# Loading batch 0's keys and queries in halves, and cutting the channel mix by free token tiles, in a fused attention and channel-mix kernel

## The chip, the core and the metric

The kernel runs on one NeuronCore of one Trainium2 chip. The core has a matrix engine (TensorE, PE in the profile; PEld is its weight load), a vector engine (VectorE, DVE), a scalar engine (ScalarE, ACT), a general engine (GpSimd, POOL) and a sync engine (SyncE, SP). Each works through its own queue of instructions in order, and they wait for each other through semaphores. In this kernel POOL's queue issues nearly all loads from memory, and SP's queue issues nearly all stores. The metric is device time in microseconds (us) of one execution, as the median of the runs shown.

## The reference

The inputs are q, k and v of shape 8 batches x 8 heads x 576 tokens x 64, phi of shape 8 x 8 x 576 x 32, and the weights of a channel mix. First comes an attention over 32 memory slots, then the channel mix over the 512 joined columns of each token:

```python
a = exp(phi - max(phi)); a = a / sum(a)                # over axis 2, the 576 tokens
k_m = einsum('bhsm,bhsd->bhmd', a, k)                  # 32 x 64 for each head
v_m = einsum('bhsm,bhsd->bhmd', a, v)
attn = softmax(q @ k_m.T / sqrt(64))                   # 576 x 32 for each head
x = join_heads(attn @ v_m)                             # batch, 576, 512
x_prev = x shifted by one token (zeros first)
xk = mu_k * x + (1 - mu_k) * x_prev                    # xr the same, with mu_r
key = relu(xk @ w_k) ** 2                              # 512 -> 1024
out = sigmoid(xr @ w_r) * (key @ w_v)                  # 1024 -> 512
```

## The kernel before

**The order of the work is written out by hand.** `PLAN` is a list of words, and the kernel emits its steps in just that order. Each engine therefore meets its instructions in the order of the words. A word such as `0:s1` is step `s1` of batch 0, `c0:3` is step 3 of the channel mix of chunk 0, and `p:wk:0-4` puts a load on POOL's queue.

**Attention of a batch.** `exp` turns phi into weights (ACT, L220). `k`, `v` or `kv` sum keys and values under them (72 matmuls with 64 or 128 columns, L232). `z` sums the weights (9 matmuls, L241). `nk` and `nv` divide by that sum (DVE). `tk` transposes the summed keys and `q0`, `q1` the queries, on PE, and DVE or ACT copies each result out of PSUM. `s0` and `s1` are the scores of two groups of four heads, with an exponential on ACT (L322, L326). `l0` to `l3` sum the exponentials and take the logarithm. `h0z` to `h3z` (or `r0z`, `r1z`) take the exponential of its negative, and `y0` to `y3` (or `w0`, `w1`) multiply (DVE, L353). Batches 0 and 1 then use `nk0`, `nk1`, `nr0`, `nr1`: the summed values times `mu` and `1 - mu` (DVE, L396). `mk0`, `mk1`, `mr0`, `mr1` build the mixed rows xk and xr for tokens 0 to 319 (half 0) or 320 to 575 (half 1) by matmuls alone (L266), and ACT and DVE share the copies into `xkT` and `xrT` (L413). Later batches compute x (`x0`, `x1`), a difference (`dd`) and the mix (`k0d`, `k2d`, `r0d`, `r2d`) on ACT and DVE. `mub` spreads `mu` over the partitions with one fp32 matmul (L195). `busy7` is seven matmuls of zeros.

**Channel mix.** The 4608 tokens are cut into nine chunks of 512. Steps 0 to 7 of a chunk are keys: four matmuls of 512 columns (L484), a relu on ACT (L488) and a square on DVE into the chunk's own `sq` tile (two buffers). Steps 8 to 11 are gates, one for each 128 tokens: four matmuls (L498), an exponential, and after every second gate a logarithm and an exponential of both (L503, L505, L506). Steps from 12 on are values: eight matmuls against `wv` (L519), a product with the gate on DVE (L521) and the stores on SP (L465). Chunk 0's values are cut into column halves, because `wv` arrives in two column halves.

**Loads.** Before the plan starts, k of batch 0 is put on POOL's queue as two halves of 64 partitions (`load_parity`, L110), then the identity matrix is made on POOL. The plan's first `p:` words add q and v of batch 0 (also two halves each), then the first half of `wk`, phi of batch 1, `wr`, k of batch 1, the second half of `wk`, q and v of batch 1, and the two halves of `wv`. Each `load` step adds a batch two ahead. From batch 6 on the queries are transposed by DMA from SP's queue (`qx`).

Of the kernel before, what the change touches and what calls it, by code (L numbers as in the profile page):

```python
# [10 lines left out]
F32 = mybir.dt.float32  # L11
BF16 = mybir.dt.bfloat16
# [6 lines left out]
    "0:exp0 0:exp1 0:k 0:z 0:mub 0:nk p:q:0 0:q0 0:q1 0:tk 0:s0 0:s1 p:v:0 p:wk:0-4 0:v 0:nk1 0:nk0 0:mu 0:nr0",  # L19
    "p:phi:1 0:l2 p:wr:0-4 0:l1 p:k:1 0:h1z 0:y1 0:l3 0:h2z 0:y2 0:l0 0:nr1 0:h3z 0:busy7 0:h0z p:wk:4-8 0:y0 0:y3",  # L20
    "0:mk1 0:mk0 0:mr0 c0:1 1:exp 0:mr1 c0:2 p:q:1 p:v:1 c0:8 c0:10 c0:11 1:k 1:z 1:nk c0:4 1:tk p:wv:0-2 c0:7 c0:5",
    "1:q0 1:q1 c0:0 c0:3 1:s0 1:v 1:s1 c0:6 1:nr0 1:l2 p:wv:2-4 1:l3 1:nk0 1:l1 0:load 1:h1z 1:l0 1:nk1 1:h3z 1:h2z",
    "1:h0z 1:y1 c0:18 c0:9 1:nr1 c0:16 1:y2 1:y0 1:y3 c0:19 c0:17 1:mk0 1:mk1 c0:15 1:load 2:exp c1:4 c1:0 1:mr0 c1:1",
    "c1:5 2:z c1:2 c1:6 2:q1 c1:8 2:q0 c0:13 2:kv 2:nk 1:mr1 2:tk 3:exp c1:3 2:s1 2:s0 c1:7 2:nv c0:14 2:load 2:l0",
    "2:l3 2:l1 c0:12 2:r0z c2:8 2:w0 2:l2 2:r1z 2:w1 3:z c1:9 3:q1 3:q0 c1:12 2:x0 c1:13 2:x1 3:kv 4:exp 3:load 3:nk",
    "3:nv c1:10 3:tk 2:dd c1:11 2:k0d 2:k2d c1:14 3:s0 3:s1 c1:15 6:load 3:l0 c2:6 3:l1 3:l3 2:r0d 3:l2 c2:0 3:r0z",
    "3:w0 3:r1z 3:w1 c2:3 c2:5 c2:1 c2:2 4:z 3:x1 2:r2d c2:4 4:kv 4:nv 4:nk 3:x0 3:dd c2:7 3:k2d c2:10 5:exp c2:9",
    "4:tk 4:q1 4:q0 3:k0d 4:load c2:12 c2:11 c2:13 c2:15 5:z 4:s1 5:kv 5:nv 4:s0 5:q0 3:r0d 5:nk 6:exp 5:q1 c3:5 4:l2",
    "c3:8 c3:6 c3:3 4:l1 5:tk 4:l0 3:r2d c3:4 4:r0z 4:l3 c3:2 c3:0 c3:1 6:z 4:r1z 6:kv 6:nv 5:s0 4:w1 5:s1 c3:7 c3:9",
    "4:w0 c2:14 6:nk 5:load 4:x1 c3:12 7:load 4:x0 6:qx c3:10 5:l3 7:exp 6:tk 4:dd 5:l1 c3:11 5:l0 5:l2 4:k2d 5:r1z",  # L30
    "4:k0d 5:r0z c3:14 c3:15 c3:13 5:w0 5:w1 c4:8 c4:1 c4:5 7:z 4:r2d 5:x0 c4:7 7:kv 6:s1 7:nk 7:nv 6:s0 c4:4 c4:0",
    "6:l2 4:r0d c4:6 5:x1 6:l0 7:tk c4:2 c4:3 6:l3 6:l1 c4:10 c4:11 7:qx 5:dd 6:r1z 5:k0d 5:k2d 6:r0z 6:w1 6:w0 c4:14",
    "c4:9 c4:15 c4:12 5:r0d 6:x0 c4:13 6:x1 6:dd c5:2 6:k0d c5:8 6:k2d c5:3 c5:1 c5:4 c5:7 c5:5 c5:6 c5:0 7:s0 7:s1",
    "c6:3 c6:6 c5:9 7:l0 7:l1 5:r2d 6:r0d c6:4 7:l2 7:r0z c6:5 7:l3 c5:13 c5:12 c6:0 7:w0 7:r1z 7:w1 c5:10 c6:8 c6:2",
    "c6:1 6:r2d c6:7 7:x0 c5:11 c5:14 7:x1 c6:9 7:dd 7:k0d 7:k2d c6:13 c6:12 c5:15 c6:10 c6:11 c8:4 c6:15 c7:8 c7:9",
    "c8:1 c8:7 c6:14 7:r2d c7:3 c8:0 7:r0d c7:5 c7:6 c7:4 c7:0 c7:1 c7:2 c7:7 c7:10 c8:3 c8:5 c8:6 c7:13 c7:11 c7:12",
    "c8:2 c7:15 c8:8 c7:14 c8:9 c8:10 c8:11 c8:12 c8:13 c8:14 c8:15",
# [3 lines left out]
PRE = "k:0 id:"  # L41
# [7 lines left out]
def kernel(  # L49
# [26 lines left out]
    NCH = NTOK // CT  # L76
# [15 lines left out]
    zeros = const.tile([128, CT], BF16, name="zeros")  # L92
# [15 lines left out]
    def load_parity(dst, src):  # L108
        for r in ROWS:
            nc.gpsimd.dma_start(out=dst[r].rearrange("p h j d -> p h (j d)"), in_=rows(src)[r])  # L110
# [33 lines left out]
    def preload(word):  # L144

        what, _, part = word.partition(":")
        if what in weights:
            dst, src = weights[what]
            f0, f1 = (int(x) * 128 for x in part.split("-"))
            nc.gpsimd.dma_start(out=dst[:, :, f0:f1], in_=src[:, :, f0:f1])  # L150
        elif what == "id":
            make_identity(nc, identity)
        else:
            n = int(part)
            if what == "phi":
                load_phi(n, nc.gpsimd)
            else:
                dst = qs[n].rearrange("p (h j) d -> p h j d", j=NJ) if what == "q" else kvs[n][:, "kv".index(what)]
                (load_rows if n else load_parity)(dst, {"q": q, "k": k, "v": v}[what][n])
# [24 lines left out]
    xr_T = big.tile([128, ND, RING], BF16, name="xrT")  # L184

    def keep_busy(n):

        ps = psum.tile([128, CT], F32, name="idle", tag="ps", bufs=8)
        for _ in range(n):
            nc.tensor.matmul(ps, lhsT=zeros[:, 0:128], rhs=zeros, start=True, stop=True,  # L190
                             skip_group_check=True)
# [14 lines left out]
    def attention(b):  # L206
# [31 lines left out]
        def esum():  # L238
            st["zps"] = ps_tile([128, 2], F32, "zps")
            for j in range(NJ):  # L240
                nc.tensor.matmul(st["zps"], lhsT=em[:, j].rearrange("p h m -> p (h m)"), rhs=ones,  # L241
                                 start=j == 0, stop=j == NJ - 1, skip_group_check=True)
            st["rz"] = work.tile([128, 2], F32, name="rz", tag="rz", bufs=3)
            nc.vector.reciprocal(st["rz"], st["zps"])

# [45 lines left out]
        def cross_q():  # L291
            for hg in range(2):
                nc.sync.dma_start_transpose(out=q_tile()[:, hg],
                                            in_=qs[b % 2][ROWS[hg]].rearrange("p n d -> p (n d)"))

# [105 lines left out]
        def mixed(w, hf):  # L401

            def go():
# [7 lines left out]
                for i in range(ND):  # L411
# [6 lines left out]
                 "z": esum, "nk": norm_k(), "nv": norm_v, "tk": tr_k(), "load": reload, "mu": load_mu, "mub": load_mu_b, "qx": cross_q}  # L418
        for i in range(2):
            steps[f"q{i}"] = tr_q(i)  # L420
            steps[f"exp{i}"] = lambda i=i: exp_phi(slice(2 * i, 2 * i + 2))
# [48 lines left out]
    def channel_mix(c):  # L470
        t0 = c * CT
        wrap = RING - t0 % RING
        pieces = [(0, CT)] if wrap >= CT else [(0, wrap), (wrap, CT)]
        st = {}

        def key(fi):
            def go():
                if "sq" not in st:
                    st["sq"] = work.tile([128, NF, CT], BF16, name="sq", tag="sq", bufs=2)
                pk = psum.tile([128, CT], F32, name="pk", tag="ps", bufs=8)  # L480
                for lo, hi in pieces:
                    c0 = (t0 + lo) % RING
                    for di in range(ND):
                        nc.tensor.matmul(pk[:, lo:hi], lhsT=wk_sb[:, di, fi * 128:(fi + 1) * 128],  # L484
                                         rhs=xk_T[:, di, c0:c0 + hi - lo],
                                         start=(di == 0), stop=(di == ND - 1))
                rl = work.tile([128, CT], BF16, name="rl", tag="rl", bufs=3)
                nc.scalar.activation(rl, pk, AF.Relu)  # L488
                nc.vector.tensor_mul(st["sq"][:, fi, :], rl, rl)  # L489
            return go  # L490

        def gate(ts):

            def go():
                pr = psum.tile([128, Dm], F32, name="pr", tag="ps", bufs=8)
                c0 = (t0 + ts * 128) % RING
                for di in range(ND):
                    nc.tensor.matmul(pr, lhsT=xr_T[:, di, c0:c0 + 128],  # L498
                                     rhs=wr_sb[:, di, :], start=(di == 0), stop=(di == ND - 1))
                if ts % 2 == 0:  # L500
                    st[ts // 2] = work.tile([128, 2, Dm], F32, name="sg", tag="sg", bufs=2)
                sg = st[ts // 2]
                nc.scalar.activation(sg[:, ts % 2], pr, AF.Exp, scale=-1.0)  # L503
                if ts % 2 == 1:
                    nc.scalar.activation(sg, sg, AF.Ln, bias=1.0)  # L505
                    nc.scalar.activation(sg, sg, AF.Exp, scale=-1.0)  # L506
            return go

        def value(ts, hs=(0,), n=1):

            def go():
                if ("o", ts) not in st:
                    st["o", ts] = work.tile([128, Dm], F32, name="o", tag="o", bufs=4)
                o = st["o", ts]
                for h in hs:
                    cols = slice(h * Dm // n, (h + 1) * Dm // n)
                    pv = psum.tile([128, Dm], F32, name="pv", tag="ps", bufs=8)
                    for fi in range(NF):
                        nc.tensor.matmul(pv[:, cols], lhsT=st["sq"][:, fi, ts * 128:(ts + 1) * 128],  # L519
                                         rhs=wv_sb[:, fi, cols], start=(fi == 0), stop=(fi == NF - 1))  # L520
                    nc.vector.tensor_mul(o[:, cols], st[ts // 2][:, ts % 2, cols], pv[:, cols])  # L521
                    store(o, t0 // 128 + ts, cols)
            return go

        if c == 0:
            values = [value(ts, (h,), 2) for ts in range(4) for h in range(2)]
        elif c == NCH - 1:
            values = [value(ts) for ts in range(3)] + [value(3, (0, 1), 2)]
        else:
            values = [value(ts) for ts in range(4)]  # L530
        return [key(fi) for fi in range(NF)] + [gate(ts) for ts in range(4)] + values


    attend = [attention(b) for b in range(B)]
    mixes = [channel_mix(c) for c in range(NCH)]
    todo = []
    for n, word in enumerate(" ".join(PLAN).split()):
# [3 lines left out]
        elif who[0] == "c":  # L541
            todo.append((n, -1, word, mixes[int(who[1:])][int(name)]))
# [34 lines left out]
```

## Time and profile before

| what | value |
|---|---|
| median of three runs | 210.34 us (209.8 to 210.54) |
| the profiled execution's own time | 210.08 us |
| span of that execution, first to last instruction | 208.3 us |
| granted TensorE clock, mean | 0.996 |
| PE busy | 193.5 us, 93% of the span |
| ACT busy | 159.7 us, 77% |
| DVE busy | 132.8 us, 64% |
| first matmul of the mixed rows of batch 0 | 19.31 us |
| first matmul of the first value | 35.95 us |
| last matmul group ends, by the chain | 204.33 us |

Times inside the execution are counted from the span's start. Busy time is the union of an engine's instructions. The profiled execution is 1.8 us longer than its span (210.08 against 208.3), and this part lies before the first and after the last instruction. The chain that ended last is followed back from the last instruction to whatever released each step. A timeline row gives a start, the time covered, the engine, the line, the operation with its tiles, the shape and a count, and in brackets the idle time ahead of it with the instruction that ended it.

### The profile page before, as it was taken

Reading aid. Unit: us, or ns where it says so; the run is one execution under the profiler, and the core shown is the slowest. Engines: PE = TensorE matmul, PEld = TensorE weight load, DVE = VectorE, ACT = ScalarE, POOL = GpSimd, SP = SyncE. Lnnn points to the kernel's source line nnn. Section 1 sums busy time; section 2 is a strip of 40 time slices with the busy share of each in tenths; the row PEclk is TensorE's granted clock in tenths of the full one; section 3 lists DMA queues with packets and bytes.
Section 4 is the critical chain, followed back from the end, with each engine's and each line's share of the span. In section 5 each row is a group of like instructions: output and inputs, shape, how many; then the busy total and the mean of one; then the engine's idle time right before and its main releaser. Section 6 shows DMA issues by size and latency. Waiting matters only on the chain.

```text
span 208.3 us, 5501 instructions
## 1 busy us (share of the span) xinstructions
PE 193.5 (93%) x2242; PEld 99.6 (48%) x2242; DVE 132.8 (64%) x331; ACT 159.7 (77%) x306; POOL 29.4 (14%) x45
## 2 busy tenths in 40 slices
PE   0379999999999999999999999999999999999992
PEld 0344454755545445465445864444444444444451
DVE  2046634866567899897769789896664925743132
ACT  3146988983998899888998999869789498656570
POOL 7653222210504004140000000000000000000000
PEclk9999999999999999999999999999999999999998
DMA  6999999999999999999997840530040262104434
GB/s 161 166 207 261 207 208 203 259 236 279 212 274 227 275 269 223 250 250 286 209 193 140 175 43 0 129 77 0 0 107 0 50 151 63 41 0 98 101 69 134
DMA packets 29273, 32.47 MB, mean 156 GB/s; under 512 B 6704, under 2 KB 24384, under 8 KB 29248
## 3 DMA queue, kind: packets, MB, share of 16 engines
q0 software_dynamic: 17392, 20.91, 53.4%
q1 hardware_dynamic: 11088, 10.37, 22.1%
q10 hardware_dynamic: 768, 0.85, 1.3%
q8 instruction: 17, 0.28, 0.5%
q14 instruction: 8, 0.07, 0.1%
HBM read 38.28 MB, written 9.44 MB: 229 GB/s over the span
## 4 chain that ended last, share of the span: by engine, by line
PE 80%; DMA 15%; POOL 2%; DVE 1%; issue 1%; POOLq 0%
PE pv L519 30%; PE pk L484 27%; PE pr L498 14%; DMA wv<-in_moe_w_v_dram 10%; DMA kv<-in_v_dram 5%; PE kvps L232 2%; PE nops L266 1%; PE zps L336 1%; PE qtps L303 1%; PE scps L322 1%; POOL kv L110 1%; DVE o L521 1%; PE mxps L266 1%; PE zps L241 1%; POOL q L110 1%
## 5 line engine op out<-in xcount | busy, mean ns | idle before, releaser
L484 PE MATMUL pk<-xkT,wk 128*128 128x512 bf16 (+1 forms) x320 | 68.3, 358 | 0.2 <-DMA wk<-in_moe_w_k_dram 0.2
L519 PE MATMUL pv<-wv,sq 128*128 128x512 bf16 (+1 forms) x328 | 66.9, 353 | 0.4 <-DMA wv<-in_moe_w_v_dram 0.4
L488 ACT ACTIVATE rl<-pk 128x512 bf16<-128x512 f32 x72 | 42.6, 606 | 11.8 <-PE pk L484 9.7
L489 DVE TENSOR_TENSOR sq<-rl 128x512 bf16<-128x512 bf16 x72 | 29.8, 423 | 31.6 <-ACT rl L488 31.1
L519 PEld LDWEIGHTS <-sq 128*128 128x128 bf16 x328 | 31.3, 98 | 30.9 <-issue 1.2
L484 PEld LDWEIGHTS <-wk 128*128 128x128 bf16 x320 | 29.9, 98 | 28.7 <-issue 1.1
L521 DVE TENSOR_TENSOR o<-sg,pv 128x512 f32<-128x512 f32 (+1 forms) x41 | 24.6, 619 | 19.7 <-PE pv L519 12.9
L498 PE MATMUL pr<-wr,xrT 128*128 128x512 bf16 x144 | 35.5, 380 | 0.0
L503 ACT ACTIVATE sg<-pr 128x512 f32<-128x512 f32 x36 | 21.2, 602 | 11.8 <-PE pr L498 8.4
L498 PEld LDWEIGHTS <-xrT 128*128 128x128 bf16 x144 | 13.5, 98 | 15.0 <-ACT xrT L413 0.3
L505 ACT ACTIVATE sg<-sg 128x1024 f32<-128x1024 f32 x18 | 19.0, 1057 | 0.6
L506 ACT ACTIVATE sg<-sg 128x1024 f32<-128x1024 f32 x18 | 19.0, 1057 | 0.6
L232 PE MATMUL kvps<-kv,em 64*32 64x128 bf16 (+1 forms) x720 | 8.7, 218 | 8.7 <-DMA kv<-in_k_dram 8.5
L365 ACT CAST x<-nops 128x320 bf16<-128x320 f32 (+1 forms) x48 | 15.6, 412 | 1.4 <-PE nops L266 1.4
L387 DVE TENSOR_SCALAR mu_d<-diff,mu 128x576 bf16<-128x576 bf16 x48 | 15.7, 369 | 0.1
L353 DVE TENSOR_TENSOR atn<-e,lz 128x576 bf16<-128x576 bf16 (+2 forms) x20 | 12.1, 633 | 2.6 <-ACT lz L346 2.4
L341 ACT ACTIVATE lz<-zps 128x320 f32<-128x320 f32 (+1 forms) x32 | 12.1, 419 | 0.7 <-PE zps L336 0.6
L232 PEld LDWEIGHTS <-em 64*32 64x32 bf16 x720 | 7.3, 92 | 10.9 <-ACT em L220 5.6
L326 ACT ACTIVATE e<-scps 128x320 bf16<-128x320 f32 (+1 forms) x32 | 10.7, 417 | 1.9 <-PE scps L322 1.9
L220 ACT ACTIVATE em<-ph 128x1152 bf16<-128x1152 f32 (+1 forms) x9 | 9.5, 1067 | 2.3 <-DMA ph<-in_phi_dram 2.3
L346 ACT ACTIVATE lz<-lz 128x576 f32<-128x576 f32 (+2 forms) x20 | 11.1, 585 | 0.2
L106 POOL DMA_DIRECT2D kv<-in_k_dram x7 | 5.2, 741 | 39.0 <-PE kvps L232 17.9
(61 smaller groups left out, 145.9 us busy)
## 6 DMA issues: line engine op xcount, KB each, us to landing
out_dram<-o SPq DMA_DIRECT2D x61, 128.0 KB, 2.4
ph<-in_phi_dram POOLq DMA_DIRECT2D x7, 576.0 KB, 20.0
kv<-in_k_dram POOLq DMA_DIRECT2D x7, 576.0 KB, 14.6
q<-in_q_dram POOLq DMA_DIRECT2D x7, 576.0 KB, 18.3
kv<-in_v_dram POOLq DMA_DIRECT2D x7, 576.0 KB, 19.7
out_dram<-o SPq DMA_DIRECT2D x18, 64.0 KB, 5.2
wk<-in_moe_w_k_dram POOLq DMA_DIRECT2D x2, 512.0 KB, 14.6
wv<-in_moe_w_v_dram POOLq DMA_DIRECT2D x2, 512.0 KB, 20.6
```

The costliest lines, as they stand in the source:

```text
L232: nc.tensor.matmul(kvps[c][g * M:(g + 1) * M], lhsT=em[ROWS[c], j, g, :], rhs=kv5[ROWS[c], parts, g, j, :], start=j == 0, stop=j == NJ - 1 ...
L365: nc.scalar.copy(st["x"][:, i, sl], pss[i])
L387: nc.vector.tensor_scalar_mul(t[:, i], st["d"][:, pr + i, :], mu1[:, o:o + 1])
L484: nc.tensor.matmul(pk[:, lo:hi], lhsT=wk_sb[:, di, fi * 128:(fi + 1) * 128], rhs=xk_T[:, di, c0:c0 + hi - lo], start=(di == 0), stop=(di = ...
L488: nc.scalar.activation(rl, pk, AF.Relu)
L489: nc.vector.tensor_mul(st["sq"][:, fi, :], rl, rl)
L498: nc.tensor.matmul(pr, lhsT=xr_T[:, di, c0:c0 + 128], rhs=wr_sb[:, di, :], start=(di == 0), stop=(di == ND - 1))
L503: nc.scalar.activation(sg[:, ts % 2], pr, AF.Exp, scale=-1.0)
L505: nc.scalar.activation(sg, sg, AF.Ln, bias=1.0)
L506: nc.scalar.activation(sg, sg, AF.Exp, scale=-1.0)
L519: nc.tensor.matmul(pv[:, cols], lhsT=st["sq"][:, fi, ts * 128:(ts + 1) * 128], rhs=wv_sb[:, fi, cols], start=(fi == 0), stop=(fi == NF - 1))
L521: nc.vector.tensor_mul(o[:, cols], st[ts // 2][:, ts % 2, cols], pv[:, cols])
```

## The change

Five things change together.

1. **k and q of batch 0 are used half by half.** The load order on POOL becomes k first half, identity, q first half, k second half, q second half, v second half, v first half, phi of batch 1, `wk` first half, `wr`, `wk` second half, k, q and v of batch 1, `wv`. The summed keys are made for one half of the partitions at a time (`k0c`, `k1c`; `v0c`, `v1c` for the values), normalised and transposed for that half (`hn0`, `ht0`, `hn1`, `ht1`), and the queries of one half are transposed by themselves (`qh0`, `qh1`, new function `tr_q_rows`), so that `s0` needs only the first halves.
2. **Chunk 0 has 576 tokens**, and its keys are cut at token 320 (`c0:3a` is tokens 0 to 319, `c0:3b` tokens 320 to 575). The other chunks are seven of 512 and a last one of 448.
3. **Gates and values are numbered by token tile** (`g:0` to `g:35`, `o:0` to `o:35`) and stand anywhere in the plan. Tiles 0 to 3 keep their column halves (`o:3a`, `o:3b`).
4. **The squared keys live in one ring** of 1152 tokens (`sq`) in place of two chunk buffers. A chunk that crosses the ring's end squares in two pieces.
5. **The plan is new from the first word to the last**, with `busy4` for `busy7`. `zeros` shrinks to 128 columns, read four times over. The options `zr` and `hold` are defined and unused.

```diff
-    "0:exp0 0:exp1 0:k 0:z 0:mub 0:nk p:q:0 0:q0 0:q1 0:tk 0:s0 0:s1 p:v:0 p:wk:0-4 0:v 0:nk1 0:nk0 0:mu 0:nr0",
-    "p:phi:1 0:l2 p:wr:0-4 0:l1 p:k:1 0:h1z 0:y1 0:l3 0:h2z 0:y2 0:l0 0:nr1 0:h3z 0:busy7 0:h0z p:wk:4-8 0:y0 0:y3",
-    "0:mk1 0:mk0 0:mr0 c0:1 1:exp 0:mr1 c0:2 p:q:1 p:v:1 c0:8 c0:10 c0:11 1:k 1:z 1:nk c0:4 1:tk p:wv:0-2 c0:7 c0:5",
-    "1:q0 1:q1 c0:0 c0:3 1:s0 1:v 1:s1 c0:6 1:nr0 1:l2 p:wv:2-4 1:l3 1:nk0 1:l1 0:load 1:h1z 1:l0 1:nk1 1:h3z 1:h2z",
...
+    "0:exp0 0:exp1 0:z p:q:0a 0:k0c 0:qh0 0:hn0 p:k:0b p:q:0b 0:ht0 0:k1c 0:hn1 p:v:0b 0:s0 0:qh1 p:v:0a 0:ht1 0:l0",
+    "0:h0z 0:s1 0:mub p:phi:1 0:l1 0:y0 0:l3 p:wk:0-4 0:h3z 0:v1c 0:h1z 0:nk1 0:v0c 0:l2 0:y3 0:nr1 0:y1 0:nr0 0:nk0",
+    "0:busy4 0:h2z p:wr:0-4 0:y2 p:wk:4-8 0:mk1 0:mr1 c0:3b 0:mr0 1:exp 0:mk0 g:2 p:k:1 c0:0b g:3 c0:2a c0:7a g:0",
+    "c0:4b 1:z c0:3a 1:k 1:nk c0:2b 7:load c0:0a c0:1a c0:4a c0:6b p:q:1 p:v:1 1:tk 1:q1 1:q0 p:wv:0-2 c0:7b c0:5a",
+    "1:s1 c0:6a 1:v 1:s0 c0:5b c0:1b 1:l0 1:l1 1:nk0 1:l3 1:h3z 1:nk1 1:l2 1:h1z 1:h2z 1:nr1 1:h0z g:1 1:y3 0:mu o:3a",
+    "1:nr0 o:2a 1:y2 1:y1 p:wv:2-4 1:y0 o:2b o:3b 1:mk1 0:load o:1b 1:mk0 6:load 1:mr0 c1:7 c1:4 2:exp c1:6 c1:5 g:4",
...
+    "5:z 3:k2d 6:qx o:10 5:kv 4:s0 4:s1 5:nk o:9 5:nv 3:r0d c3:6 4:l1 4:l2 c3:4 c3:1 3:r2d 4:l0 c3:0 6:exp 5:q0 5:q1",
+    "g:12 5:tk 4:l3 c3:5 c3:3 4:r0z c3:7 6:z 6:kv 4:r1z 5:s1 4:w0 5:s0 4:w1 c3:2 g:13 6:nk 6:nv o:11 6:tk 4:x0 o:12",
+    "4:x1 g:14 5:l0 4:dd 5:load 5:l1 g:15 5:r0z 7:exp 5:l2 4:k2d 4:k0d 5:l3 5:r1z o:13 5:w0 o:15 o:14 c4:7 c4:0 7:z",
...
-PRE = "k:0 id:"
+PRE = "k:0a id:"
...
+    STARTS = (0,) + tuple(range(S, NTOK, CT))
...
+    sq = big.tile([128, NF, 2 * S], BF16, name="sq")
...
+        def tr_q_rows(hg):
+            def go():
+                r = ROWS[hg]
+                for i in range(2):
+                    ps = ps_tile([128, NJ, QR], BF16, "qtps")
+                    for n in range(NJ):
+                        n0 = 2 * (NJ * i + n)
+                        nc.tensor.matmul(ps[:, n], rhs=identity[r, r], is_transpose=True,
+                                         lhsT=qs[b % 2][r, n0:n0 + 2, :].rearrange("p n d -> p (n d)"),
+                                         start=True, stop=True, skip_group_check=True)
+                    (nc.scalar.copy if i else nc.vector.tensor_copy)(q_tile()[:, hg, NJ * i:NJ * (i + 1)], ps)
+            return go
...
+        def key(fi, lo, hi):
+            def go():
+                pk = psum.tile([128, CT], F32, name="pk", tag="ps", bufs=8)[:, :hi - lo]
+                cut = min(hi, -(lo + 1) // RING * -RING)
+                for p0, p1 in ((lo, cut), (cut, hi)) if cut < hi else ((lo, hi),):
...
                 nc.scalar.activation(rl, pk, AF.Relu)
-                nc.vector.tensor_mul(st["sq"][:, fi, :], rl, rl)
+                cut = min(hi, -(lo + 1) // (2 * S) * (-2 * S))
+                for p0, p1 in ((lo, cut), (cut, hi)) if cut < hi else ((lo, hi),):
+                    p = p0 % (2 * S)
+                    nc.vector.tensor_mul(sq[:, fi, p:p + p1 - p0], rl[:, p0 - lo:p1 - lo], rl[:, p0 - lo:p1 - lo])
...
+        if c == 0:
+            return {f"{fi}{'ab'[hf]}": key(fi, sl.start, sl.stop) for fi in range(NF) for hf, sl in enumerate(HALVES)}
...
+    def gate(t):
...
+            if t % 2 == 0:
+                gated[t // 2] = work.tile([128, 2, Dm], F32, name="sg", tag="sg", bufs=2)
...
+    def value(t, hs=(0,), n=1):
...
+                    nc.tensor.matmul(pv[:, cols], lhsT=sq[:, fi, p:p + 128],
+                                     rhs=wv_sb[:, fi, cols], start=(fi == 0), stop=(fi == NF - 1))
+                nc.vector.tensor_mul(o[:, cols], gated[t // 2][:, t % 2, cols], pv[:, cols])
+                store(o, t, cols)
```

## The prediction

> **What bounds the kernel now.** I read the page's busy times and slices first, then the chain that ended last in order of time, then the timeline of the first 40 us.
>
> ```profile
> PE 193.5 (93%) x2242; PEld 99.6 (48%) x2242; DVE 132.8 (64%) x331; ACT 159.7 (77%) x306; POOL 29.4 (14%) x45
> PE   0379999999999999999999999999999999999992
> DMA  6999999999999999999997840530040262104434
> ```
>
> PE works in every slice from the fourth to the last but one. What isn't PE work lies in the first three slices (16 us) and the last. The transfers fill theirs from the second slice to the 22nd.
>
> ```profile
> 4.94 9.61 DMA kv<-in_v_dram
> 14.55 0.28 issue
> 14.83 20.98 DMA wv<-in_moe_w_v_dram
> 35.81 0.14 issue
> 35.95 1.03 PE pv L519 x8
> ...
> 39.17 1.14 DVE atn L353 x3
> ...
> 41.03 0.41 PE mxps L266 x13
> ...
> 197.39 6.94 PE pv L519 x40
> 204.33 0.02 issue
> 204.35 0.42 DVE o L521
> ```
>
> The chain is loads until the first value at 35.95, passes through DVE near 39 to 41, and is PE alone from 41.03 to 204.33. So a microsecond won or lost before 41 moves the end by a microsecond.
>
> ```profile
> 13.38 0.74 POOL L106 DMA_DIRECT2D kv<-in_v_dram  x1 [0.67 <-DMA kv<-in_v_dram]
> 13.59 0.73 PE L322 MATMUL scps<-qT,kmT 64*32 64x320 bf16 x16 [0.39 <-DVE kmT L283]
> 14.83 0.88 POOL L150 DMA_DIRECT2D wv<-in_moe_w_v_dram  x1 [0.71 <-DMA kv<-in_v_dram]
> 16.46 2.92 PE L190 MATMUL idle<-zeros 128*128 128x512 bf16 x7
> 19.31 2.12 PE L266 MATMUL mxps<-atn,vm 32*64 32x256 bf16 x64
> 23.56 2.75 PE L498 MATMUL pr<-wr,xrT 128*128 128x512 bf16 x12
> 25.38 0.74 POOL L106 DMA_DIRECT2D q<-in_q_dram  x1 [2.35 <-DMA kv<-in_k_dram]
> 35.95 1.03 PE L519 MATMUL pv<-wv,sq 128*128 128x256 bf16 x8 [0.44 <-DMA wv<-in_moe_w_v_dram]
> ```
>
> PE fills the time from 16.46 to 19.31 with zeros while the softmax is finished. POOL's rows date the landings: each load waits until the load eight places earlier has landed. So the six halves of batch 0 land near 7.0, 8.7, 10.3, 11.7, 13.1 and 14.6, wk's first half at 17.9, wr at 22.0, batch 1's k at 25.1, wk's second half at 27.4, q at 30.3, v at 33.1, wv's halves at 35.8 and 38.5. These come from the starts at 7.24, 8.92, 10.52, 11.97, 13.38, 14.83, 18.16, 22.29, 25.38, 27.99, 30.80, 33.62, 36.34 and 39.00, less 0.2 to 0.5 us.
>
> [...] the zeros' weight loads stand 0.43 us apart [...], four later keys take 0.864 us in the chain (216 ns each). [...] Here halves of 0.59 MB in fp32 land every 1.5 us, 390 GB/s[...]. [...]
>
> **The change, part by part.**
>
> *Halves.* In the new order first-half k lands at 7.0, first-half q at 8.7, second-half k at 10.3, second-half q at 11.7, v at 13.1 and 14.6. PE is in order, and `s0` stands behind `k1c`, so it starts near 10.9 (10.3 plus 0.4 of sums), against 13.59. `s1` waits for the second q: 0.55 of transposes, 0.64 of the ACT copy, 0.2 of signals, so 13.3. Then `mub` takes 1.25 on PE, and DVE can start at 14.9. Ahead of the mixing its queue holds two `mu` copies (0.83), four products `y` (0.43 + 0.49 twice) and four `vm` (0.31 each): 3.9 us. The first `vm` that mixing needs is ready at 18.3, the last `y` at 18.8. So mixing starts at 18.3, not 19.31: 1.0 us sooner. The three zeros fewer (1.3 us) only fill this wait, so they earn nothing by themselves.
>
> *What the mixing waits for then.* Before, PE put a key between the mixed halves, and its first gate came at 23.56 after all the mixing and two keys (1.73). Now `g:2` comes after all the mixing and half a key (0.44). DVE must first copy out 2 + 2 tiles of 256 columns (0.41 each: 19.1 to 20.75), the square of `c0:3b` that waits for ACT's relu (to 21.35), then two tiles of 320 (0.45 each): `g:2` starts near 22.4. wr, landing at 22.0, would allow it no earlier than that. Thus it starts 1.15 sooner with 1.29 less done: 1.0 us of the head start is used up here. ACT's exponential of batch 1 (1.18) stands between the copies too, and hides behind DVE.
>
> *From there to the first value.* Gates 4 x 0.864 = 3.46, keys 16 pieces at 0.547 or 0.437 = 7.87 less the 0.44 done = 7.43, batch 1's k, z, tk, q, s, v, l 0.75 + 0.20 + 0.23 + 0.74 + 0.40 + 0.75 + 0.48 = 3.55, and `mu` (before it lay under the softmax) 0.27: 14.71. Before, the same sum was 2.59 + 5.18 + 3.55 = 11.32 and the trace took 11.95 to the wv wait, of which about 0.48 stood on the second wk half at 27 to 28. I keep 0.15. First value: 22.4 + 14.71 + 0.15 = 37.25. In the old kernel 35.95 plus what the new one has done more (64 tokens of keys 0.86, a gate 0.86) is 37.67. That is 0.4 us sooner. The waits that vanish are 0.44 for wv and 0.48 for wk.
>
> *Loads in time?* The second wk half now goes ahead of batch 1's k: landings 24.3 and 27.3. The steps need it at 25.1, k at 27.7, q at 31.2, v at 33.7, wv at 37.25 and 39.0: 0.4 to 1.4 us late enough, no more. So a faster start could bring at most 0.4 us more before k is waited for.
>
> *39 to 41.* The old chain's DVE passage has 0.25 us of PE idle or waiting. Four values (3.5 us) now stand ahead of batch 1's mixing, so I take 0.25 off.
>
> *Ring and cuts.* Chunks 2, 4 and 6 square in two pieces: 24 instructions x 0.16 = 3.7 us on DVE, at least nothing, at most that. DVE waits 31.1 us for relus in all, which hides it; without that cover it is 1.2 us in each of three stretches. Chunk 0's 16 relus take 6.6 us on ACT for 5.5. Keys of tokens 1152 earlier are read well before they are overwritten in the plan (the last such value stands ahead of each chunk's first key), so the ring adds no wait. Values and gates keep their counts and shapes.
>
> *The rest of the plan.* PE's work from the first mixing on is the same within 0.1 us by columns. ACT holds about 152 us against PE's 185 there, as before. The tightest new place is `c6:6`, 0.9 us of PE work ahead of `o:25`: it is read seventh of eight, 1.3 us later, and ACT has 8.0 us of work for PE's 8.7. The last values, gates and stores end as before, 4.0 us after the last matmul. I count nothing.
>
> Sum: 0.4 + 0.25 = 0.7 us off the profiled execution's 210.08 (span 208.3 to 207.6), which is 209.4. The median stands 0.26 above that execution: 209.6.
>
> **Rivals.**
>
> *The loads set the pace.* If mixing and `g:2` go a microsecond better (a shorter DVE queue), batch 1's k at 27.3 still caps the gain at 0.7 + 0.4: 209.2. If instead the loads land 0.5 us later than read off, all margins are gone and 0.1 to 0.2 us are left: 210.2. For it: six loads within 1.4 us of their use. Against: the bytes ahead of each load are the same or fewer, k apart.
>
> *The other side: the DVE queue ahead of `g:2`.* Place: `mub`, four `vm` and four `y` in one stretch, then copies behind a square that waits for PE and ACT. Each microsecond there goes to the end one for one. Break-even is `g:2` at 23.1. If second-half q lands at 12.7[...], it comes at 24.1 and the time is 1.0 us above before: 211.3. For it: the sum has nothing to spare, POOL makes the identity ahead of q's first half (0.5 us). Against: the transfers have a backlog by then.
>
> *SP.* `6:qx` now follows the issue of batch 6's q, which took 16.4 us to land. Stores from `o:10` on queue behind it. They leave near 103.7, `o:13` needs the buffer at 109.6. q later than 102 stops DVE; PE holds out for 5.6 us more. So it costs something only from a landing at 107 on; 2 us then.
>
> *Nothing happens.* The order of starts did change, so equal time would be a cancellation, counted under the first rival.
>
> **How the numbers follow.** The likeliest case has 0.5 (its own range 209.2 to 210.0), the cap 0.13, late loads 0.15, the DVE queue or SP 0.22. A change of 0.3% (0.63 us) is about what a measurement can tell from none. The likeliest gives 0.32 of its half to faster and 0.17 to the same, the cap all to faster, late loads 0.12 to the same, the slow cases 0.2 to slower: faster 0.46, same 0.30, slower 0.24. The range takes in the cap (with 0.7 us for loads sooner than read off) and the slow case: 208.5 to 211.3.
>
> **What would show it.** `s0` near 11, mixing near 18.3, `g:2` near 22.4, the first value at 37.3 with 0.2 us or less of load waits, no PE gap over 0.3 us from 41 on, last matmul near 203.6. Wrong, if PE waits within 41 to 200, if `g:2` is past 23.1[...].

## The result and the profile after

The changed kernel takes 210.52 us (median of 20 runs, 210.0 to 211.64) against 210.07 us (209.5 to 210.57) for the kernel before: a ratio of 1.0026 with a 95% interval of 1.0012 to 1.004. It is about 0.5 us slower. The forecast was 209.6 us, 0.7 below the three runs from which it started and 0.5 below the 20 runs here. The profiled execution took 210.57 us with a span of 208.8 us; that of before took 210.08 and 208.3.

The page of the changed kernel, with the columns of the page shown before:

```profile
PE 193.3 (93%) x2250; PEld 102.9 (49%) x2271; DVE 134.8 (65%) x364; ACT 160.6 (77%) x314; POOL 29.4 (14%) x45
PE   0599898999999999999999999999999999999991
DMA  6999999999999999999997940341006253002525
q8 instruction: 18, 0.29, 0.6%
```

PE starts earlier (5 in the second slice for 3, 9 in the third for 7), and its total work is the same. The last line is new to this text. It is a transfer queue that carries instructions, 18 packets of 0.29 MB in all, so 16 KB each; the old kernel's page has 17. The page counts it on the same 16 transfer engines as the loads, which fill the DMA row up to the 23rd slice (120 us).

The chain that ended last, in order of time (start, us, what):

```profile
7.05 14.92 DMA wr<-in_moe_w_r_dram
...
30.98 0.63 PE qtps L339 x36
31.61 0.81 PE pk L520 x6
32.43 0.84 issue
33.27 0.43 PE pk L520 x2
...
37.78 0.15 PE psmu L208
37.94 3.60 PE pv L565 x32
...
52.34 0.72 PE kvps L237 x71
53.07 0.44 issue
53.51 0.21 PE kvps L237
```

The chain is loads until wr lands at 21.97 and PE alone from there. Two pieces in it are neither: 0.84 us before 33.27 and 0.44 us before 53.51, called "issue", time in which PE waited for nothing that the profile shows. The first lies inside a group of four matmuls that add up one key, the second before the last of the 72 matmuls of one batch's sums. In both places the matmul ahead belongs to the same step, and the paused one waits for no semaphore, so nothing in the program makes PE wait there. The view of what PE waited for (total, times, longest) has them too; these are its rows two to five:

```profile
PE qtps L326 <- DMA q<-in_q_dram: 1.0, 2, 0.8
PE pk L520 <- issue: 0.8, 1, 0.8
PE pr L543 <- DMA wr<-in_moe_w_r_dram: 0.7, 1, 0.7
PE kvps L237 <- issue: 0.4, 1, 0.4
```

The timeline of PE up to the first value:

```profile
10.26 0.45 PE L358 MATMUL scps<-qT,kmT 64*32 64x320 bf16 x4
...
18.05 1.08 PE L288 MATMUL mxps<-atn,vm 32*64 32x256 bf16 x32
...
22.11 1.02 PE L543 MATMUL pr<-wr,xrT 128*128 128x512 bf16 x3 [0.69 <-DMA wr<-in_moe_w_r_dram]
...
33.27 0.43 PE L520 MATMUL pk<-xkT,wk 128*128 128x320 bf16 x2 [0.84 <-issue]
...
37.87 3.67 PE L565 MATMUL pv<-wv,sq 128*128 128x256 bf16 x32
```

The first scores start at 10.26, mixing at 18.05 and `g:2` at 22.11, each somewhat ahead of the forecast. The first value comes at 37.87, 0.62 us behind it; the first pause of 0.84 us is more than all of that.

**Where the two pauses lie in the program.** I counted PE's instructions in the order of its program, from the first weight load on as place 0. A weight load and its matmul are two places, and a wait that stands in PE's list by itself is one. The first instruction after the first pause is a matmul at place 959, after the second one a matmul at place 1727. 959 + 65 is 4 x 256, and 1727 + 65 is 7 x 256, so the pauses lie 768 places apart.

Of the packets of the instruction queue, two start between those of the two pauses (36.94 and 43.00 us), so 768 places are three packets. By this count a packet brings a block of 256 instructions, and 16 KB for 256 are 64 bytes each. Counted on, the packets fit one block after the other. The first of the run (14.47 us) is the one for place 447, and the new list of 4552 places begins one block more, at 4543, than the old one of 4494: hence 18 packets for 17. Both pauses thus fall where a block ends. Why my count is 65 places off the multiples of 256 the trace doesn't tell.

The packets that belong to the pauses start at 30.94 and 51.16 us, and PE goes on 2.33 and 2.35 us after that. The transfers of the 0.2 us from 30.9 on (packets, MB, share of 16 engines) show the first of them among the loads:

```profile
q0 software_dynamic: 63, 0.04, 125.9%
q8 instruction: 1, 0.02, 27.9%
```

**Why in the new kernel.** PE stopped at these two edges 1.49 and 1.91 us after the next block's packet had started, and went on at 2.33 and 2.35. The windows of 6 us up to the two pauses, after (busy us and, in brackets, recorded instructions of PE and PEld, then the other engines):

```profile
27.60:33.60 6.00, 5.16 (x138) 3.88 (x137) 4.42 (x16) 4.82 (x12) 1.53 (x3) 1.00 1.32 204
47.70:53.70 6.00, 5.56 (x153) 3.32 (x152) 4.24 (x12) 5.36 (x10) 0.76 (x1) 1.00 1.16 265
```

and before, for the same two blocks:

```profile
27.20:33.20 6.00, 5.77 (x87) 2.68 (x86) 3.33 (x10) 5.44 (x9) 1.50 (x2) 1.00 1.28 204
49.00:55.00 6.00, 5.87 (x146) 3.14 (x145) 4.21 (x12) 3.41 (x9) 2.85 (x4) 1.00 1.17 249
```

Keys of chunk 0 cut at token 320 are matmuls of 320 and 256 columns in place of 512, and the plan puts batch 1's sums and transposes (72 and 36 short matmuls) between them. PE runs 138 matmuls in the first window for 87 before. From edge to edge the two blocks last 5.9 and 4.3 us with their pauses in them, against 6.8 and 5.2 us before, where the new block was there, by the same 2.35 us after its packet's start, 1.0 and 0.7 us before PE came to the edge.

### The profile page after: what moved, and what is told of

Read it like the earlier page. It is cut to its first block, busy times and chain, and to the rows that moved or that the text cites. A ratio compares the mean times of both kernels' runs of the same rounds, so it can differ in the third digit from the quotient of the medians.

```text
span 208.8 us, 5585 instructions
## 1 busy us (share of the span) xinstructions
PE 193.3 (93%) x2250; PEld 102.9 (49%) x2271; DVE 134.8 (65%) x364; ACT 160.6 (77%) x314; POOL 29.4 (14%) x45
## 3 DMA queue, kind: packets, MB, share of 16 engines
q0 software_dynamic: 17392, 20.91, 53.6%
## 4 chain that ended last, share of the span: by engine, by line
PE 86%; DMA 7%; POOL 3%; issue 2%; DVE 0%; POOLq 0%; DVEq 0%
PE pk L520 30%; PE pv L565 30%; PE pr L543 15%; DMA wr<-in_moe_w_r_dram 7%; PE kvps L237 3%; PE zps L372 2%; PE qtps L339 2%; PE nops L288 1%; POOL kv L110 1%; PE scps L358 1%; PE zps L247 1%; POOL q L110 1%; PE mxps L288 1%; DVE o L567 0%; PE ktps L301 0%
## 5 line engine op out<-in xcount | busy, mean ns | idle before, releaser
L520 PE MATMUL pk<-xkT,wk 128*128 128x512 bf16 (+4 forms) x347 | 69.3, 341 | 1.6 <-issue 0.8
L565 PE MATMUL pv<-wv,sq 128*128 128x512 bf16 (+1 forms) x323 | 65.3, 353 | 0.2
L528 DVE TENSOR_TENSOR sq<-rl 128x512 bf16<-128x512 bf16 (+5 forms) x104 | 32.7, 341 | 36.3 <-ACT rl L524 35.7
L524 ACT ACTIVATE rl<-pk 128x512 bf16<-128x512 f32 (+3 forms) x80 | 43.2, 564 | 15.7 <-PE pk L520 15.1
L520 PEld LDWEIGHTS <-wk 128*128 128x128 bf16 x352 | 32.9, 98 | 29.8 <-issue 1.5
L567 DVE TENSOR_TENSOR o<-sg,pv 128x512 f32<-128x512 f32 (+1 forms) x41 | 24.8, 619 | 14.8 <-PE pv L565 9.2
L548 ACT ACTIVATE sg<-pr 128x512 f32<-128x512 f32 x36 | 22.0, 611 | 5.7 <-PE pr L543 5.1
L401 ACT CAST x<-nops 128x256 bf16<-128x256 f32 (+1 forms) x48 | 15.7, 420 | 5.0 <-PE nops L288 4.8
L413 DVE TENSOR_TENSOR diff<-x 128x1024 bf16<-128x1024 bf16 (+1 forms) x18 | 9.0, 554 | 1.8 <-ACT x L401 1.8
L107 POOL DMA_DIRECT2D kv<-in_k_dram x7 | 5.2, 743 | 30.9 <-PE kvps L237 22.2
```

The lines of the kernel that those rows point to most:

```text
L401: nc.scalar.copy(st["x"][:, i, sl], pss[i])
L520: nc.tensor.matmul(pk[:, p0 - lo:p1 - lo], lhsT=wk_sb[:, di, fi * 128:(fi + 1) * 128], rhs=xk_T[:, di, p0 % RING:p0 % RING + p1 - p0], sta ...
L528: nc.vector.tensor_mul(sq[:, fi, p:p + p1 - p0], rl[:, p0 - lo:p1 - lo], rl[:, p0 - lo:p1 - lo])
L548: nc.scalar.activation(sg[:, t % 2], pr, AF.Exp, scale=-1.0)
L565: nc.tensor.matmul(pv[:, cols], lhsT=sq[:, fi, p:p + 128], rhs=wv_sb[:, fi, cols], start=(fi == 0), stop=(fi == NF - 1))
L567: nc.vector.tensor_mul(o[:, cols], gated[t // 2][:, t % 2, cols], pv[:, cols])
```

## The experiments

The theory: *PE ran out of its own instructions*, and what decides is where in its list a dense stretch falls, since by the count above the blocks are cut every 256 places. The rivals are that the pauses belong to the steps (something they wait for that the trace does not name), and that the slowness comes from the plan. The main tool is a step of n two-column matmuls of zeros ahead of everything else. They run in the first microseconds, in which PE has nothing to do (in the changed kernel its first matmul starts at 6.43), and move every later instruction by 2n places. Besides that they use PE earlier and take one PSUM buffer more, which the run with n = 1 does as well. The lines of such a kernel stand 6 or 8 further on (L528 for L520).

```
+    def short_matmuls(n):
+        ps = psum.tile([128, CT], F32, name="short", tag="ps", bufs=8)
+        for _ in range(n):
+            nc.tensor.matmul(ps[:, 0:2], lhsT=zeros[:, 0:128], rhs=zeros[:, 0:2], start=True, stop=True, skip_group_check=True)
...
-    "0:exp0 0:exp1 0:z p:q:0a ...
+    "0:short14 0:exp0 0:exp1 0:z p:q:0a ...
```

Ratios are to runs of the kernel before that were taken along: median 209.89 us for `after_short14`, `before_short14`, `after_short26` and `after_short14_whole`, 209.98 for `after_again` and the two with more loads, 209.87 for the others.

**28 places on** (the diff above).

> The changed kernel with 14 two-column matmuls of zeros put first on PE, where PE has nothing to do until 6.4 us. Each is two PE instructions (a weight load and a matmul), so all later PE instructions stand 28 places further on. Fetch theory: the two PE gaps of the changed kernel (0.84 us at 33.27, in the middle of a group of four matmuls, and 0.44 us at 53.5) are PE out of instructions; the page counts 18 instruction packets of 16 KB, 256 PE instructions each, and a gap belongs to a place in the instruction stream counted in 256s. 28 places on, the ends of the blocks fall where more time of long matmuls lies between them: both gaps go, at most 0.5 us comes up near 38, and the time is 0.8 to 1.2 us below the changed kernel, 209.3 to 209.7, so below the kernel before by 0.2 to 0.4%. Place theory (the gaps belong to these steps: late keys, a semaphore that the profile doesn't show, a bank of PSUM): both gaps stay at the same steps, and the time stays at a ratio of 1.0026 to the kernel before.

Measured: 208.63 us (208.42 to 209.72, 6 runs), ratio 0.9941 [0.9919, 0.9962]. Fourteen matmuls of nothing make the kernel 1.9 us faster, more than the 0.8 to 1.2 expected, and it beats both kernels. PE's waits in its profile, all of 0.3 us and more:

```profile
PE zps L253 <- ACT em L231: 5.6, 1, 5.6
PE short L201 <- DVE zeros L125: 1.0, 1, 1.0
PE qtps L332 <- DMA q<-in_q_dram: 0.7, 1, 0.7
PE pr L551 <- ACT xrT L455: 0.5, 1, 0.5
PE ktps L307 <- DVE kbd L280: 0.3, 1, 0.3
```

No "issue" is left. And the two steps in its timeline, with the same matmuls as before the pauses of the changed kernel:

```profile
31.80 1.03 PE L528 MATMUL pk<-xkT,wk 128*128 128x256 bf16 x7
32.78 0.33 PE L364 MATMUL scps<-qT,kmT 64*32 64x320 bf16 x8
...
51.43 0.80 PE L243 MATMUL kvps<-kv,em 64*32 64x128 bf16 x72
```

Compared step by step, the n-th weight load of one against that of the other, it is 0.13 us later than the changed kernel up to the first pause, 0.84 us earlier right after it, 1.48 us earlier after the second, and 1.51 us earlier at the end. So by this count the pauses cost about 0.97 and 0.64 us, something more than the idle time shown, and 1.6 of the 1.9 us are theirs.

**The old kernel, 28 places on.**

```
-    "0:exp0 0:exp1 0:k 0:z 0:mub ...
+    "0:short14 0:exp0 0:exp1 0:k 0:z 0:mub ...
```

> The kernel before with the same 14 two-column matmuls put first on PE. Fetch theory: from the trace of the kernel before, the time from one block's end to the next is shortest, 6.4 us, for the block that ends near 55 us, and it has no gap there; 28 places on, this stretch shrinks to 5.2 us, as the dense sums of batch 2 (144 instructions in 0.73 us) move wholly into it. A PE gap of 0.5 to 1.2 us appears near 53 to 55, and the time rises by as much: ratio 1.002 to 1.006. Place theory: nothing changes, ratio 1.000 within 0.001. The same edit is to make one kernel faster and the other slower only by the fetch theory.

Measured: 210.95 us (210.49 to 211.57), ratio 1.0046 [1.0031, 1.0061]. The same step that speeds the new kernel up slows the old one down. In its timeline:

```profile
53.55 0.33 PE L328 MATMUL scps<-qT,kmT 64*32 64x320 bf16 x8
54.12 0.33 PE L328 MATMUL scps<-qT,kmT 64*32 64x320 bf16 x8 [0.24 <-ACT em L226]
```

The old kernel without the short matmuls runs these 16 as one group. Here they are torn apart at place 1727 again, 2.33 us after a packet's start at 51.80, and the step comparison jumps by 0.55 us. The profile writes the idle time to an exponential on ACT (em) that ended at 53.93. The scores don't read it, and in the old kernel's trace the same scores ran from 53.69 on while it was still going; the place and the packet tell what the pause was. The pause is half of the 1.1 us by which the median rises. It is all of the difference between the two profiled executions (210.59 and 210.08); what the slower ones have besides, no profile shows.

**52 places on.**

```
+    "0:short26 0:exp0 0:exp1 0:z p:q:0a ...
```

> The changed kernel with 26 of the two-column matmuls, 52 places on. Fetch theory: the gaps at 33 and 53 go, but the block that ends near 37 to 38 us now has 4.9 us from the end of the one before, as little as the worst of the changed kernel, so one gap of 0.8 to 2 us appears there, near the last scores of batch 1 and ahead of the first value; the time is between the changed kernel less 0.5 us and the changed kernel plus 0.7 us. Place theory: gaps at the same two steps as in the changed kernel, ratio 1.0026.

Measured: 209.29 us (208.89 to 209.97), ratio 0.9967 [0.9952, 0.9982]. PE's timeline:

```profile
35.78 0.65 PE L378 MATMUL zps<-e,sumh 128*128 128x320 bf16 x4 [0.82 <-ACT rl L532]
```

The pauses at 33 and 53 us are gone, and a new one of 0.82 us stands at a step that had none, at place 1215, once more 65 short of a multiple of 256. The profile puts it down to a relu on ACT, but that had ended at 35.38, 0.40 us before PE went on. The block's packet starts at 33.27, 2.51 us before. By steps this kernel is 0.5 us ahead of the changed one before the first pause, gains 1.0 us at 33, loses 1.0 at 35.8 and gains 0.64 at 53.5. Pause and place came as expected. The time is 1.2 us below the changed kernel, where at most 0.5 was expected.

**2 places on, and the changed kernel as it is.** `after_short1` has a single short matmul, `after_again` none.

> One two-column matmul of zeros first, so the program is moved by 2 places only, while all that is new in after_short14 besides the places is there: an early matmul, and the matmul banks moved on by one. Place theory (PE waits for its next block of 256 instructions): the blocks end where they did, within 2 places, so PE stands still near 33.3 us for 0.7 to 1.0 us and near 53.5 us for 0.3 to 0.8 us, as in the changed kernel; ratio to the kernel before 1.001 to 1.004. Rival (what helped was the early matmul or the other banks): no such waits and a ratio of 0.992 to 0.996, as with 14.

Measured: 209.52 us (209.19 to 210.49), ratio 0.9989 [0.9977, 1.0001], below what I expected. In its timeline:

```profile
32.77 0.33 PE L364 MATMUL scps<-qT,kmT 64*32 64x320 bf16 x8
...
52.58 0.23 PE L243 MATMUL kvps<-kv,em 64*32 64x128 bf16 x2 [0.37 <-issue]
```

The second pause is there, at place 1727. The first is not: its packet starts at 29.66 us, 1.3 us sooner than in the changed kernel, for a step that comes at the same time, and PE passes the edge 2.6 us after it. So neither account holds in full. For the first pause this run doesn't exclude that an early matmul by itself helps; for the second it does, as that pause is there. By these two profiles the place decides whether a block is short of time, and the packet's own start, which came 1.3 us sooner here, whether it is late. What moves it I can't tell: the trace shows when a packet starts, not what starts it. The times come in two groups, nine runs from 209.19 to 209.55 and five from 209.86 to 210.49, as if a pause came and went; only one of them was profiled.

> The changed kernel once more, with nothing altered. Two places are 0.1 us from no pause in its first trace, so single executions may fall on either side. Place theory: the profile shows the pause near 33.3 us (0.7 to 1.0 us) or, if the block's packet starts at least 0.5 us sooner against its step, none there; times in two groups some 0.8 us apart, as in after_short1. Ratio 1.001 to 1.004 by the first runs.

Measured: 210.88 us (210.26 to 210.94, 5 runs), ratio 1.0038 [1.0018, 1.0059]. The second profile of the changed kernel repeats the first within 0.1 us: PE is idle for 0.92 us before 33.23 and for 0.46 us before 53.49, with packets at 30.85 and 51.20. In this kernel the pauses are no accident of one execution.

**The short matmuls late.** To take one pause away and leave the other, the 14 matmuls stand between two keys of chunk 1.

```
-    ... 6:load 1:mr0 c1:7 c1:4 2:exp c1:6 c1:5 g:4",
+    ... 6:load 1:mr0 c1:7 0:short14 c1:4 2:exp c1:6 c1:5 g:4",
```

> The changed kernel with the 14 two-column matmuls not first but between two keys of chunk 1, near 44.7 us. They cost 0.5 us of PE there. Place theory: everything up to 44.7 us is as in the changed kernel, the pause of 0.84 us near 33.3 us stays, and the pause of 0.44 us near 53.5 us goes, for the block now ends at another step: against the changed kernel step by step +0.5 us from 44.7, then 0.0 from 54 us, ratio to the kernel before 1.001 to 1.004. Rival (the pauses come from what the steps wait for, not from their places): both pauses stay, all steps from 44.7 us on are 0.5 us late, ratio 1.0045 to 1.006.

Measured: 210.03 us (209.62 to 210.64), ratio 1.0006 [0.9998, 1.0015], a little under the 1.001 to 1.004 expected. Its timeline:

```profile
33.19 0.43 PE L528 MATMUL pk<-xkT,wk 128*128 128x320 bf16 x2 [0.96 <-issue]
...
52.55 0.80 PE L243 MATMUL kvps<-kv,em 64*32 64x128 bf16 x72
```

The first pause stays and the second is gone. By steps the kernel is 0.08 us ahead of the changed one before 44.9 us, 0.27 behind after the short matmuls, and 0.38 ahead after 53.5. The rival, that the pauses go with their steps, would have kept both. No matmul was put first here, so an early one isn't what takes the second pause away.

**The old kernel, 96 places on**, where by the old trace no block is short of time.

```
+    "0:short48 0:exp0 0:exp1 0:k 0:z 0:mub ...
```

> The kernel before with 48 two-column matmuls first (96 places on), some 1.8 us of PE work in the first 6 us, in which PE has nothing else. Place theory: by the times at which the old trace passes these places, no block is used up in less than 6.8 us, so PE never waits for instructions: no pause without a semaphore over 0.2 us after 25 us, ratio 0.998 to 1.002 (the pauses that 28 places brought, 0.55 us near 54 us, are gone again). Rival (short matmuls cost the old kernel something in any number): 1.004 or more, as with 14 or worse.

Measured: 210.15 us (209.62 to 210.89), ratio 1.002 [1.0011, 1.003]. No pause at a block's end is left (its waits of 0.72 us at 14.90 and 0.50 at 35.97 are for v and wv, and end ahead of an edge): the 16 scores near 53.6 are one group again, and the step comparison ends 0.1 us ahead of the old kernel. The median is nevertheless 0.3 us above it, at the edge of what I expected, and no view shows from what.

**The halves undone**, in the plan with 14 short matmuls: old words and old load order for batch 0, everything after `0:mk1` as changed, four zeros kept.

```
-    "0:short14 0:exp0 0:exp1 0:z p:q:0a 0:k0c 0:qh0 0:hn0 p:k:0b p:q:0b 0:ht0 0:k1c 0:hn1 p:v:0b 0:s0 0:qh1 p:v:0a 0:ht1 0:l0",
...
+    "0:short14 0:exp0 0:exp1 0:k 0:z 0:mub 0:nk p:q:0a p:q:0b 0:q0 0:q1 0:tk 0:s0 0:s1 p:v:0a p:v:0b p:phi:1 p:wk:0-4 0:v 0:nk1 0:nk0",
+    "0:l2 p:wr:0-4 0:l1 0:h1z 0:y1 0:l3 0:h2z 0:y2 0:l0 0:nr1 0:nr0 0:h3z 0:busy4 0:h0z p:wk:4-8 0:y0 0:y3",
...
-PRE = "k:0a id:"
+PRE = "k:0a k:0b id:"
```

> The changed kernel with 14 short matmuls and batch 0's front put back as before: k, q and v in two halves each in the old load order, sums, transposes and scores for both halves at once; the rest of the plan is the changed one. PE has as many instructions ahead of the mixing as with the halves, so the blocks end at the same places. My account of the halves: mixing starts near 19.3 instead of 18.05, the first gate near 23.3 instead of 22.1, and the time is 0.9 to 1.3 us above the run with halves. Rival, that the loads set the pace (wr at 22.0, batch 1's k at 27.3, wv at 35.8): the first gate comes at most 0.5 us later and the time is 0.0 to 0.4 us above the run with halves.

Measured: 210.47 us (209.53 to 211.25), ratio 1.0014 [0.9998, 1.0031], 1.84 us above `after_short14`, more than I had worked out. Its timeline:

```profile
19.44 0.49 PE L294 MATMUL mxps<-atn,vm 32*64 32x256 bf16 x4
20.84 1.06 PE L294 MATMUL mxps<-atn,vm 32*64 32x256 bf16 x28 [0.90 <-DVE atn L395]
...
24.12 0.61 PE L551 MATMUL pr<-wr,xrT 128*128 128x512 bf16 x1
...
39.38 3.67 PE L573 MATMUL pv<-wv,sq 128*128 128x256 bf16 x32
```

Mixing starts 0.8 us later than in `after_short14` (18.62), and then waits 0.90 us for the attention weights from DVE. The first value comes at 39.38 for 37.02. So the halves do bring mixing and first value forward. How much they are worth is less sure. The profiled execution is the slowest of the 14 (211.25; five lie from 209.53 to 209.9, nine from 210.14 to 211.25), and 0.45 us of its delay comes with the first gate, whose first matmul at 24.12 takes 0.61 us for 0.38. The 1.84 us is an upper end also because the old words stand in front of a plan that wasn't made for them.

**Zeros of two columns.**

```
-    "0:busy4 0:h2z p:wr:0-4 ...
+    "0:short4 0:h2z p:wr:0-4 ...
```

> after_short14 with its four 512-column matmuls of zeros ahead of the mixing made two columns wide, so that the count of instructions stays. My step said that the zeros only fill a wait. If so, mixing starts where it did (18.6 us) and takes the same time, and the ratio is that of after_short14 within 0.001 (0.993 to 0.995). Rival [...]: [...] mixing and the copies end up to 0.8 us later, ratio 0.995 to 0.998.

Measured: 208.97 us (208.67 to 210.2), ratio 0.9957 [0.9943, 0.9971]. The value itself lies where the rival put it (0.995 to 0.998), but the interval overlaps that of `after_short14`. Six of the seven executions lie from 208.67 to 209.65. The seventh, at 210.2, is the profiled one:

```profile
22.37 1.86 PE L551 MATMUL pr<-wr,xrT 128*128 128x512 bf16 x4 [0.23 <-PE mxps L294]
```

In it the first gate's four matmuls take 1.86 us where they take 1.02 in `after_short14`, and by steps 1.2 us are lost within three microseconds. Ahead of them PE had been idle for 0.47 us at 16.90 (place 447, a block's end again, 2.62 us after its packet), 0.48 at 18.09 and 0.35 at 19.07. So in most executions the zeros fill a wait, and in the profiled one their absence goes with a slow first gate (1.86 us). That it is the cause isn't shown: `after_short14_whole` has its four zeros and a slow first gate too, after the wait of 0.90 us at 20.84. Both idled ahead of the gate, but `after_short1` idled 1.32 us just before its own and ran it in 1.02.

**More loads where there are none.** From 107 us on POOL's loads are done in `after_short14`, the transposing loads on SP end near 120, and from 123 us on the instruction packets start before PE begins the block ahead. 22 loads of keys into buffers that nobody reads are added to `after_short14`, four at a time and then one at a time.

```
+    def extra_loads(nd, nl):
+        places = [kvs[1][:, 0], kvs[1][:, 1], kvs[0][:, 0], kvs[0][:, 1]][:nd]
+        for i in range(nl):
+            load_rows(places[i % nd], k[i % 8])
...
-    ... 7:tk c4:4 7:qx ...
+    ... 7:tk 0:extra4x22 c4:4 7:qx ...
```

> after_short14 with 22 more loads of 1.2 MB from about 107 us on, over key and value buffers that nobody reads any more, four of them outstanding at a time. In after_short14 the blocks of PE's instructions whose packets start at 116.5, 123.6 and 145.6 us start 1.7 us after, 2.4 us before and 3.3 us before PE begins the block ahead of the one they bring (places 3519, 3775 and 4031 of PE's list). Theory (the transfer engines serve the block after what the loads have queued there): for as long as the extra loads run these packets start 2 to 5 us later against those steps. No pause of PE from it, since these blocks last 11 us and more. Rival (a block always comes at the same distance after its request, and what differs early is only PE's pace): unchanged within 0.5 us. Time: nothing known, as the stores share the transfer engines; it isn't what is asked.

> The same 22 loads into one buffer, so that only one is outstanding at a time. If the delay of a block comes from how much the loads have queued, it is 0 to 2 us against after_short14's steps here, clearly less than with four outstanding; if any running load delays it alike, it is as there, 2 to 5 us.

Measured, packet start against the step at which PE begins the block ahead (minus: earlier):

| place | as it is | four outstanding | one outstanding |
|---|---|---|---|
| 3519 | +1.7 | +1.2 | +1.1 |
| 3775 | -2.4 | -1.3 | -2.7 |
| 4031 | -3.3 | -0.8 | -3.3 |
| 4287 | -4.4 | -1.7 | -2.6 |

A place in the first column is the one at which the block ahead begins. The extra loads began only at 115.6 us, so the first row has none of them. In the others, four outstanding loads delay the packet by 1.1, 2.5 and 2.7 us; one outstanding load by nothing, nothing and 1.7. The first 1.1 is less than the 2 us I expected. PE's pace between these steps is the same in all (24.8 us between the last two with four loads as with none), so the added loads delay the blocks, and more when four are queued than with one. This rests on one execution of each and three packets. That the times are 220.4 and 264.98 us has another reason: with four, batch 7's transposed queries came late, and with one, the last of the 22 loads was issued only at 256.22 us, long after PE's work.

```profile
PE scps L369 <- DMA qT<-q: 10.2, 1, 10.2
```

## Why the prediction was wrong

I take the prediction's steps in order. Without the pauses its sum comes out, as shown at the end.

*Halves*: held in time. s0 at 10.26 (10.9), mixing at 18.05 (18.3). What mixing waited for last was a product `y` on DVE (atn, to 18.00), not `vm`. Two sums are 0.2 us larger than their terms (10.3 + 0.4 is 10.7, and s1's come to 13.1, not 13.3), which did no harm.

*What the mixing waits for then*: the time was right, 22.11 for 22.4. The limit was the transfer, not DVE: PE waited 0.69 us for wr, which landed at 21.97 (22.0). That the time fits is in part luck, as the two limits lay within 0.4 us; in `after_short14`, where mixing starts at 18.62, the copies came last, and the gate at 22.24. The rival "the DVE queue ahead of `g:2`", with its break-even at 23.1, falls.

*From there to the first value*: **this is the step that failed first**, in the words "I keep 0.15". The work was right: 22.11 + 14.71 is 36.82, and `after_short14`, which has no pause, reaches the first value 37.02, 14.78 us after its gate at 22.24. In the changed kernel 0.84 us of pause stands in this stretch. I took the 0.15 from what the old kernel's own sum left over. It holds no such pause, because in the old trace every block was there, by the same 2.35 us, at least 0.7 us before PE came to its edge, and so the prediction put the coming of PE's instructions at nothing without a reason from the new plan.

*Loads in time?*: held for k, q, v and wv, which PE does not wait for. The one load whose landing I did not list was PE's own instructions. The rival "the loads set the pace" named k, q and v of batch 1 and wv; PE waited for none of them.

*39 to 41*: held. From the first value to the last matmul the old kernel took 168.38 us, less 1.72 for a gate and 64 tokens of keys done before it in the new one, 166.66. The new one took 204.65 - 37.87 = 166.78, of which 0.44 is the second pause. 0.32 us were gained for the 0.25.

*Ring and cuts*: the price of a further piece, 0.16 us as I had estimated it, was right. Squares of 512, 320, 192 and 64 columns take 424, 323, 253 and 188 ns, so about 155 ns beside the columns. No PE wait of 0.3 us or more shows after 54 us, neither for a square nor for what the rival "SP" feared.

*The rest of the plan*: **the second step that failed**, "I count nothing" and "no PE gap over 0.3 us from 41 on". The gap at 53.51 is 0.44 us, again PE's own instructions. After it there is none.

The sum for the profiled execution: 37.67 less 37.03 (37.87 without the pause) is 0.64 us gained up to the first value, 0.32 after it, and 0.17 lost between the last matmul and the end (5.92 for 5.75): 0.79 us, where 0.7 was forecast. Against it stand 0.84 + 0.44 = 1.28, and the kernel is 0.49 us slower in that pair of executions, 0.45 in the medians. The plan itself, moved by 28 places, is 1.26 us faster than the kernel before. That is more than 0.79: by steps the pauses cost 1.6 us and not 1.28, so the plan's gain without them was 1.1 to 1.3 us, and the forecast of 0.7 was somewhat low.

*Three zeros fewer*: "earn nothing by themselves" held in most executions. With none, one execution of seven had a slow gate; with four, `after_short14_whole` had one as well. Whether seven would have kept it fast was not tried.

What stays open: what moved the packet at 29.66 by 1.3 us; half of the loss of the old kernel's median with 14 short matmuls and the 0.2% with 48; how many of the changed kernel's executions have both pauses; what makes the first gate slow.

## What to carry to other kernels

When a change packs many short matmuls together while loads fill the transfer engines (90% or more in the DMA row here), count the matmuls and weight loads from start to each dense stretch: here the two blocks that lasted 5.9 and 4.3 us, pauses included, were followed by a late one, and 28 or 52 places more at the head of the program, where PE idles, were worth 0.9 and 0.6%. Read "issue" within a group of equal matmuls as a sign of it, and distrust a releaser named at such a place. Before a plan is judged against another, try each at two or three offsets, or the comparison is between offsets: by offset alone the new plan's medians here went from 208.63 to 210.88 us and the old one's from 209.87 to 210.95.

## What the runs showed of the hardware

- PE's instructions came in packets of 16 KB for 256 places, about one block ahead, while the transfer engines carried the loads. The pauses after 25 us, eight in six profiles, all end at a place 65 short of a multiple of 256 (959, 1215 or 1727).
- PE went on 2.3 to 2.5 us after the start of the packet in all of them.
- Up to 105 us, while loads ran, the packets started between 0.6 us before and 4.2 us after PE began the block ahead, and no two of them less than 5.8 us apart. From 120 us on, with few transfers, they started 0.4 to 4.4 us before that. There the blocks also last longer (22 to 28 us), so the transfers alone don't explain that difference; the runs with added loads show their part.
- The pauses show as 0.24 to 0.96 us of idle PE each; by steps they cost up to 0.3 us more (0.55 where 0.24 shows).
